# A spectral layer and a rational MLP on one core: batch 0's x in halves of 48 rows, its results stored per two chunks, a fifth chunk of batch 1 ahead of the main loop

## The chip, the cores and the metric

One core of a Trainium2 chip runs the whole kernel. The metric is device time in microseconds (us), from a launch of the program. Engines: PE (TensorE, the matmuls), ACT (ScalarE), DVE (VectorE), POOL (GpSimd) and SP (SyncE, here only an issuer of DMAs). "Idle before, releaser" in a row is how long the engine stood still ahead of an instruction, and whose end let it go on.

## The reference

```python
X = np.fft.rfft(x, axis=1)                    # x: 4 batches x 3008 x 256, float32
Yr = Xr @ w_r - Xi @ w_i + b_r                # 256 x 256 weights
Yi = Xr @ w_i + Xi @ w_r + b_i
Y  = sign(Y) * max(|Y| - 0.01, 0)             # real and imaginary part apart
y  = np.fft.irfft(Yr + 1j * Yi, n=3008, axis=1)
h  = y.reshape(12032, 256) @ w_in             # 256 x 2048
P  = a0 + a1*h + a2*h^2 + a3*h^3
Q  = 1 + |b0|*|h| + |b1|*h^2
out = (P / (Q + 1e-6)) @ w_out                # 2048 x 256
```

## The kernel before

The transform of length 3008 is split into 47 x 64. For a batch, `f1_task` (L160 ff.) does the 47-point part in eight chunks: a chunk of x (`xin`, 128 partitions, of which 0 to 47 hold group g=0 and 64 to 111 group g=1) goes through eight matmuls (L165), ACT copies the half of group 0 and DVE that of group 1 out of PSUM into a tile `a` (`copy`, L148 and L150), and `send` (L190) stores the tile to the staging tensor `s1` in DRAM, which the trace calls `s`. `f2_task` (L223) reads s1 back as `b_all` (batch 0) or `bt` (batches 1 to 3) and does the 64-point part; `m_task` (L252, L259) mixes with w_r and w_i and thresholds; `i1_task` (L277) starts the inverse transform and stores to a second staging tensor `s2` (row `s<-zt`); `i2_task` (L323) ends it from tiles `ct` and leaves its result as `xsh` (ACT, L326) and `xsl` (DVE, L334).

The program has two parts. The **prologue** (L506 to the line `pro_stack.close()`) is batch 0's transform up to i1, with the conversion of the MLP's weights, which come as float64 words (`raw_win`, `raw_wsp`; `convert`, L490 to L502), woven in by hand through the lists `HC`, `HM` and `HF`. `warm` issues matmuls on an unused tile (L517); `WARM` of them stand between batch 0's f1 and f2. At the end of the prologue four f1 chunks of batch 1 are done: one in the last round of the loop over p, three in the loop over `HF`, each followed by some steps of `convert`. Their stores (`sends`, then `direct`) stand in SP's queue behind the last loads of ct.

The **main loop** runs over 208 units. A unit is h (`g1_mm`, L357), the rational function on ACT (v, s, t in L389 to L393, y in L398 and L400), DVE (t in L405 and L406, g in L414 and L426, v in L416) and POOL, with a DMA that adds s to v (L391), and the second product `g2_mm` (acc, L447) of the unit three back. The transforms of batches 1 to 3 are laid between the units by a planner: `fft_tasks` gives each task a cost in us, and a task is taken when what has been spent falls behind a budget.

All of the kernel's order is written by hand (`manual_schedule`): each engine and each DMA queue works in the order of issue. An instruction waits on semaphores for what it reads, and for old users of a buffer that it writes. The DMAs that SP and ACT issue take eight completion counters (DMAHW0 to DMAHW7) in turn, and a DMA waits for the last one on its counter.

The tiles of the prologue lie in pools (`pro`, `pro2`, `pro3`) that are closed before the main loop; the loop's pools `mx` (xsh, xsl) and `mp` (v, s, t, y, g) take over their memory, so a first write there waits for the last users of what lay there.

Of the kernel before, what the change touches and what calls it, by code (L numbers as in the profile page):

```python
# [28 lines left out]
WARM = 27  # L29
HC = (0, 0, 3, 3, 3, 3, 3, 3, 3, 3, 3, 3)  # L30
HM = (0, 0, 3, 4, 3, 4, 3, 4, 3, 4, 3, 4, 8, 0)
HF = (2, 3, 2)
I2Q = (5, 6)
SIZES = (5,) * 14 + (4,) + (5,) * 10 + (4,)
C0 = float(np.float32(1.0) + np.float32(1e-6))
# [59 lines left out]
def spectral_moe(ctx, tc, t, out):  # L95
# [37 lines left out]
    def load_x(b, c):  # L133
        if b == 1 and c in (2, 3):
            xt = pro3.tile([128, 4, D], F32, tag=f"x{c}", name="xin", bufs=1)
        elif b == 1 and c >= 6:
            xt = sm.tile([128, 6, D], F32, tag="x", name="xin", bufs=2)[:, :4]
        elif b == 0 and c >= 2:
            xt = const.tile([128, 4, D], F32, tag=f"win{c}", name="xin")
        else:  # L140
            xt = sm.tile([128, 4, D], F32, tag="xin", name="xin")
        rows = 112 if b == 0 and c < 2 else 128
        nc.sync.dma_start(out=xt[:rows], in_=t["x"][b, c, :rows])
        xin[b, c] = xt

    def copy(eng, out, in_):
# [12 lines left out]
    def f1_task(b, c, pos):  # L159
        if pos == 0:  # L160
            s1[b] = dram.tile([NK, 2, NG, NJ, D], F32, tag="s1", name="s1")
        pts = [bank(b, "f1" if g else "") for g in range(NG)]
        for g, h in ((0, 0), (1, 1), (0, 1), (1, 0)):
            r = slice(64 * g, 64 * g + 48)
            nc.tensor.matmul(out=pts[g][64 * h:64 * h + 64], lhsT=f1[r],  # L165
                             rhs=xin[b, c][r, 2 * h:2 * h + 2, :].rearrange("p j d -> p (j d)"), start=True, stop=True)
        yield
        whole = None
        if b == 0:
            whole = const.tile([128, NG, 2, D], F32, tag=f"wsp{c}", name="a")  # L170
        elif early:
            whole = pro.tile([128, NG, 2, D], F32, tag="a" if pos < 3 else "wt", name="a", bufs=3 if pos < 3 else 1)
        elif b > 1:
            whole = sm.tile([128, 3, 2, D], F32, tag="x", name="a", bufs=2)[:, :NG]
        parts = [sm.tile([128, 2, D], F32, tag="a", name="a", bufs=3) if whole is None else whole[:, g] for g in range(NG)]
        for g in range(NG):
            copy(g if early else b == 1, parts[g].rearrange("p j d -> p (j d)"), pts[g])
        yield
        del xin[b, c]
        if b == 1 and c < 2:  # L180
            hold.append(lambda: load_x(b, c + 4))
        elif b > 1 and c + 2 < NJ // 4:
            load_x(b, c + 2)
        dst = s1[b].rearrange("k c g j d -> (k c) g j d")

        def send():
            for h in range(2):
                r, o = slice(64 * h, 64 * h + 48), slice(4 * c + 2 * h, 4 * c + 2 * h + 2)
                if whole is not None:
                    nc.sync.dma_start(out=dst[:, :, o], in_=whole[r])  # L190
                else:
                    for g in range(NG):
                        nc.sync.dma_start(out=dst[:, g, o], in_=parts[g][r])

        send() if b == 0 or direct or not early else sends.append(send)

    sends = []
    direct = []
    b_t = {}
# [258 lines left out]
    def drain(g):  # L458
        for _ in g:
            pass  # L460

    def fft_tasks(b):
        turns = (0, 1, 2, 3, 6, 7, 4, 5) if b == 1 else range(8)
        ts = [(0.87, 2, 2, f1_task(b, c, pos), 0) for pos, c in enumerate(turns)]
        ts += [(0.0, 0, 0, load_first(b), 0)] + [(0.0, 0, 0, iter(()), 0)]
        np_ = NK // 2
        for p in range(np_ + 2):
            if p < np_:
                ts.append((0.86, 1, 1, f2_task(b, p), 1))
            if p == 0:  # L470
                ts.append((0.0, 0, 0, iter(()), 0))
            if 1 <= p <= np_:
                ts += [(1.43, 1 - k, k, m_task(b, p - 1, k), 0) for k in range(2)]
            if p >= 2:
                ts.append((0.87, 1, 1, i1_task(b, p - 2), 0))
        return ts
# [29 lines left out]
    with tc.manual_schedule():  # L506
        nc.vector.memset(cb, 1.0)
        nc.scalar.dma_start(out=f1, in_=t["f1"])
        nc.scalar.activation(out=cb, in_=cb, func=ACTF.Abs_reciprocal_sqrt)
        b_all = [pro3.tile([128, 6, D], F32, tag=f"b{z}", name="b_all", bufs=1) for z in range(4)]  # L510
        nc.vector.memset(offset[:, 0], 0.0)
# [5 lines left out]
                nc.tensor.matmul(out=pt, lhsT=idle[:, :128], rhs=idle, start=True, stop=True)  # L517

        warm(9)
        for c in range(8):  # L520
            load_x(0, c)
        sel = pro.tile([4, 130], F32, tag="sel", name="sel", bufs=1)
        bsb = pro.tile([4, D], F32, tag="bsb", name="bsb", bufs=1)
        blo = pro.tile([4, D], F32, tag="blo", name="blo", bufs=1)
        eye = pro.tile([128, 128], F32, tag="eye", name="eye", bufs=1)

        def load_small():
            nc.sync.dma_start(out=sel, in_=t["sel"])
            for k, nm in enumerate(("b_r", "b_i")):
                nc.sync.dma_start(out=bsb[2 * k:2 * k + 2, :],  # L530
                                  in_=t[nm].rearrange("(o d) -> o d", o=1).to_broadcast([2, D]))
            nc.sync.dma_start(out=eye, in_=t["minus"])

        def prepare_small():
            nc.vector.memset(v32(selr), 0.0)
            nc.vector.memset(v32(bias), 0.0)
            yield
            nc.vector.tensor_copy(selr[:4], sel[:, 0:128])
            nc.scalar.activation(out=minus, in_=eye, func=ACTF.Copy)
            bhi = bias[:4, 0]  # L540
            nc.vector.tensor_copy(bhi, bsb)
            yield
            nc.vector.tensor_tensor(out=blo, in0=bsb, in1=v32(bhi), op=ALU.subtract)
            nc.vector.tensor_scalar(out=bsb, in0=v32(bhi), scalar1=sel[:, 128:129], scalar2=None, op0=ALU.mult)
            yield
            for k in range(2):
                nc.vector.scalar_tensor_tensor(out=bias[:4, k], in0=blo, scalar=sel[:, 129:130], in1=bsb, op0=ALU.mult, op1=ALU.add)
# [41 lines left out]
        def load_f2(a, z):  # L589
            nc.sync.dma_start(out=f2[:, a:z], in_=f2_src[:, a:z])  # L590
# [8 lines left out]
            nc.sync.dma_start(out=wt, in_=t["w"])  # L599
            wts.extend(wt[:, k] for k in range(2))  # L600

        load_small()
        small_steps = prepare_small()
        for c in range(8):
            drain(f1_task(0, c, c))
            if c >= 4:
                next(small_steps, None)
        load_f2(0, 8)
        load_wt()
        prepare_mix()  # L610
        load_all(0, 2)
        load_all(2, 2)
        load_all(4, 2)
        load_f2(8, 12)
        np_ = NK // 2
# [5 lines left out]
        for p in range(np_ + 3):  # L621
            if p < np_:
                f2g = f2_task(0, p)
                next(f2g)
                next(f2g)
            if p < 2:
                warm(2 - p, "m")
            flush()
            if p == np_:
                load_first_c(0, 16)  # L630
            if p == np_ + 2:
                load_first_c(16, NK - 2)
            if p == 0:
                more_raw(2)
            elif p == 1:
                load_all(12, 6)
            elif p == 2:
                load_f2(12, 24)
                nc.sync.dma_start(out=ca, in_=t["a"].rearrange("(o d) -> o d", o=1).to_broadcast([128, 4]))
                nc.sync.dma_start(out=cb, in_=t["b"].rearrange("(o d) -> o d", o=1).to_broadcast([128, 2]))  # L640
                nc.sync.dma_start(out=i2, in_=t["i2"])
            if p >= 1:
                more_raw(2)
            if p == 3:
                load_g1(8, 16)
            elif p == 4:
                load_all(18, 6)
            elif p == 5:
                load_g1(16, NK)
            if 6 <= p < 12:  # L650
                load_x(1, (0, 1, 2, 3, 6, 7)[p - 6])
            if p < np_:
                convert(HC[p])
            if p == np_ + 1:
                drain(i1_task(0, p - 3))
                root()
            if 2 <= p < np_ + 2:
                drain(m_task(0, p - 2, 0))
                drain(m_task(0, p - 2, 1))
                convert(HM[p])  # L660
            if p < np_:
                drain(f2g)
            if p == np_ + 1:
                drain(first.pop(0)[3])
            if p >= 3 and p != np_ + 1:
                drain(i1_task(0, p - 3))
            if p == 8:
                for k, nm in enumerate(("b_r", "b_i")):
                    for z in range(2):
                        nc.sync.dma_start(out=offset[64 * k:64 * k + 64, z],  # L670
                                          in_=t[nm].rearrange("(o d) -> o d", o=1).to_broadcast([64, D]))
# [148 lines left out]
```

## Time and profile before

| | us |
|---|---|
| median of 3 runs | 1435.2 (1434.85 to 1436.17) |
| the profiled execution, its own time | 1433.67 |
| its span, first to last instruction | 1431.9 |
| PE busy | 1400.0 (98%) |
| DVE busy | 1295.3 (90%) |
| ACT busy | 1133.3 (79%) |
| POOL busy | 669.0 (47%) |

The span is 1.8 us shorter than the execution's own time, and that is 1.5 us under the median of the runs. Busy shares are means over the whole span; the first 155 us look different from the rest, and all that is changed lies there.

### The profile page before, as it was taken

What the parts mean: (1) busy time and instruction counts of PE and PEld (TensorE: products, weight loads), DVE (VectorE), ACT (ScalarE), POOL (GpSimd) and SP (SyncE); (2) the same over time, 40 slices, a digit from 0 to 9 for tenths busy, and PEclk for the clock granted to TensorE, in tenths of its full rate; (3) what the DMA queues carried; (4) which work ended last, traced back from release to release, by engine and by line L of the source; (5) the groups of instructions that cost most, each with busy time, mean ns of one, the idle gap of its engine ahead of it and who ended that gap; (6) DMA issues with size and microseconds to landing.
All of it is one profiled execution on the core that took longest, in us unless ns stands there. A gap on an engine that the chain in (4) does not pass through costs nothing.

```text
span 1431.9 us, 20413 instructions
## 1 busy us (share of the span) xinstructions
PE 1400.0 (98%) x7552; PEld 1227.9 (86%) x7553; DVE 1295.3 (90%) x1302; ACT 1133.3 (79%) x1435; POOL 669.0 (47%) x444
## 2 busy tenths in 40 slices
PE   6989999999999999999999999999999999999997
PEld 2976899998888999999878999999988888888886
DVE  2778889999889889999889899999999999999998
ACT  2767777878888778878788787888788998889985
POOL 0443344454454444444444444455455555555553
PEclk8999999999999999999999999999999999999999
DMA  8968455546586554564686455554555555555543
GB/s 283 385 197 198 99 110 125 107 102 143 134 212 150 104 122 100 105 147 98 132 227 148 97 126 113 114 121 96 103 119 114 108 109 105 112 109 108 109 84 79
DMA packets 85079, 191.66 MB, mean 134 GB/s; under 512 B 8748, under 2 KB 40468, under 8 KB 84980
## 3 DMA queue, kind: packets, MB, share of 16 engines
q0 software_dynamic: 29952, 98.58, 38.7%
q1 hardware_dynamic: 54884, 91.75, 19.4%
q8 instruction: 60, 0.98, 0.3%
q14 instruction: 39, 0.32, 0.1%
q10 hardware_dynamic: 144, 0.03, 0.0%
HBM read 54.28 MB, written 37.49 MB: 64 GB/s over the span
## 4 chain that ended last, share of the span: by engine, by line
PE 77%; DVE 11%; issue 8%; DMA 2%; ACT 2%; SPq 1%; DVEq 0%; ACTq 0%
PE h L357 30%; PE acc L447 29%; PE pft L259 7%; PE pi L323 3%; DVE t L405 3%; DVE v L416 3%; PE pft L223 3%; PE pft L277 2%; PE pft L165 1%; DVE g L414 1%; DMA s<-a 1%; PE pm L259 1%; DVE t L406 1%; DVE e L497 1%; DVE e L495 1%
## 5 line engine op out<-in xcount | busy, mean ns | idle before, releaser
L447 PE MATMUL acc<-g,wsp 128*128 128x470 f32 (+1 forms) x2496 | 561.1, 373 | 4.7 <-DVE g L426 4.7
L420 POOL TENSOR_TENSOR t<-t,v 128x940 f32<-128x940 f32 (+1 forms) x206 | 477.3, 2317 | 139.5 <-DVE v L416 126.8
L447 PEld LDWEIGHTS acc<-g,wsp 128*128 128x128 f32 x2496 | 468.4, 189 | 64.1 <-DVE g L426 6.0
L357 PE MATMUL h<-xsh,win 128*128 128x470 f32 (+1 forms) x1664 | 433.6, 382 | 5.4 <-DVE t L406 4.9
L391 POOL DMA_DIRECT2D v<-s x208 | 183.8, 884 | 535.5 <-issue 498.3
L357 PEld LDWEIGHTS h<-xsh,win 128*128 128x128 f32 x1664 | 303.9, 190 | 60.9 <-PE acc L447 9.6
L389 ACT ACTIVATE v<-h 128x940 f32<-128x940 f32 (+1 forms) x208 | 196.1, 943 | 150.7 <-PE h L357 144.5
L414 DVE SCALAR_TENSOR_TENSOR g<-t,small,y 128x940 fp32r<-128x940 f32 (+1 forms) x208 | 253.6, 1219 | 53.1 <-ACT y L400 52.8
L405 DVE TENSOR_TENSOR t<-t,h 128x940 f32<-128x940 f32 (+1 forms) x208 | 231.3, 1112 | 24.9 <-ACT t L393 23.2
L406 DVE SCALAR_TENSOR_TENSOR t<-t,small,h 128x940 f32<-128x940 f32 (+1 forms) x208 | 245.1, 1179 | 7.4
L426 DVE SCALAR_TENSOR_TENSOR g<-t,small,y 128x940 fp32r<-128x940 f32 (+1 forms) x208 | 244.1, 1174 | 0.1
L357 PE MATMUL h<-xsl,win 128*128 128x470 f32 (+1 forms) x832 | 242.4, 373 | 0.0
L416 DVE SCALAR_TENSOR_TENSOR v<-v,g 128x940 f32<-128x940 f32 (+1 forms) x208 | 231.6, 1113 | 0.0
L393 ACT ACTIVATE t<-h,small 128x940 f32<-128x940 f32 (+1 forms) x208 | 215.7, 1037 | 0.0
L398 ACT ACTIVATE y<-v 128x940 f32<-128x940 f32 (+1 forms) x208 | 205.6, 989 | 9.7 <-DMA v<-s 9.4
L400 ACT ACTIVATE y<-y 128x940 f32<-128x940 f32 (+1 forms) x208 | 204.1, 981 | 2.4
L390 ACT ACTIVATE s<-h 128x940 f32<-128x940 f32 (+1 forms) x208 | 195.2, 939 | 0.0
L357 PEld LDWEIGHTS h<-xsl,win 128*128 128x128 f32 x832 | 156.3, 188 | 20.1
L259 PE MATMUL pft<-wrh,x 128*128 128x256 f32 x288 | 76.5, 287 | 0.2 <-ACT pft L150 0.2
L259 PE MATMUL pft<-wih,x 128*128 128x256 f32 x288 | 75.3, 283 | 0.1
L323 PEld LDWEIGHTS pi<-small,ct 96*128 96x128 f32 x512 | 65.0, 192 | 5.9 <-ACT a L150 3.1
L323 PE MATMUL pi<-small,ct 96*128 96x94 f32 x512 | 64.2, 272 | 2.3 <-DMA ct<-s 2.2
(88 smaller groups left out, 1065.8 us busy)
## 6 DMA issues: line engine op xcount, KB each, us to landing
v<-s POOLq DMA_DIRECT2D x192, 470.0 KB, 4.6
xin<-in_x SPq DMA_DIRECT2D x30, 512.0 KB, 6.2
s<-zt SPq DMA_DIRECT2D x48, 256.0 KB, 3.5
out_t<-ob SPq DMA_DIRECT2D x48, 235.0 KB, 4.4
s<-a SPq DMA_DIRECT2D x56, 192.0 KB, 4.3
ct<-s SPq DMA_DIRECT2D x20, 480.0 KB, 5.6
bt<-s SPq DMA_DIRECT2D x36, 256.0 KB, 3.8
v<-s POOLq DMA_DIRECT2D x16, 376.0 KB, 4.2
```

Of the source, the lines that this page charges most:

```text
L259: nc.tensor.matmul(out=pt[:, k, :], lhsT=l, rhs=r, start=False, stop=n == len(ops) - 1, skip_group_check=True)
L357: nc.tensor.matmul(out=h[:, i, :w], lhsT=l, rhs=r, start=k == 0, stop=k == len(halves) // FU - 1)
L393: nc.scalar.activation(out=d["t"], in_=h, func=ACTF.Identity, scale=rate["a3"], bias=ca[:, 2:3])
L398: nc.scalar.activation(out=d["y"], in_=d["v"], func=ACTF.Square, bias=C0)
L400: nc.scalar.activation(out=d["y"], in_=d["y"], func=ACTF.Abs_reciprocal_sqrt)
L405: nc.vector.tensor_tensor(out=tt, in0=tt, in1=h, op=ALU.mult)
L406: nc.vector.scalar_tensor_tensor(out=tt, in0=tt, scalar=ca[:, 1:2], in1=h, op0=ALU.add, op1=ALU.mult)
L414: stt(out=hi, in0=tt, scalar=ca[:, 0:1], in1=y, op0=ALU.add, op1=ALU.mult)
L416: stt(out=v, in0=v, scalar=C0, in1=v32(hi), op0=ALU.add, op1=ALU.mult)
L420: nc.gpsimd.tensor_tensor(out=tt[:, :cut], in0=tt[:, :cut], in1=v[:, :cut], op=ALU.subtract)
L426: stt(out=lo, in0=tt, scalar=ca[:, 0:1], in1=y, op0=ALU.add, op1=ALU.mult)
L447: nc.tensor.matmul(out=acc[n][e][:, :w], lhsT=l, rhs=r, start=begun[n] == 1 and seen[e] == 1, stop=begun[n] == UB and seen[e] == 3 * FU)
```

## The change

1. Batch 0's x is loaded as sixteen halves of 48 rows (192 KB each), twelve from SP's queue and four (group 1 of chunks 0 to 3) from ACT's, ahead of ACT's table load. Before, it came as eight loads of 112 or 128 rows from SP.
2. Batch 0's results are stored per two chunks, group by group, from 48 partitions with 4 KB a row: eight stores on SP (group 1) and eight on ACT (group 0). Before there were sixteen on SP with rows of 2 KB. The host lays x out to fit.
3. The small inputs `sel`, `b_r`, `b_i` are loaded by ACT after the f1 stage, and what DVE makes of them follows then. `eye` is loaded at p == 2, and ACT's copy of it to `minus` moves to p == 6.
4. Behind the stores SP's order becomes f2 table 0 to 3, b_all 0 and 1, wt, b_all 2 and 3, f2 table 4 to 7, b_all 4 and 5, f2 table 8 to 11; `prepare_mix` comes after f2 of p == 0.
5. A fifth f1 chunk of batch 1 is done in the loop over HF (2, 2, 2, 1). Its tile `a` lies in pool `pro3` under the tag "x".
6. The planner's cost of an f1 task is 0.95, and in the last two chunks of batch 1 both copies are ACT's.

```diff
-HF = (2, 3, 2)
+HF = (2, 2, 2, 1)
...
-        rows = 112 if b == 0 and c < 2 else 128
-        nc.sync.dma_start(out=xt[:rows], in_=t["x"][b, c, :rows])
+        if b == 0:
+            for g in range(NG):
+                r = slice(64 * g, 64 * g + 48)
+                (nc.scalar if g and c < 4 else nc.sync).dma_start(out=xt[r], in_=t["x"][b, c, r])
+        else:
+            nc.sync.dma_start(out=xt, in_=t["x"][b, c])
...
+        pair, s = divmod(c, 2)
         if b == 0:
-            whole = const.tile([128, NG, 2, D], F32, tag=f"wsp{c}", name="a")
+            if not s:
+                a_t[:] = [const.tile([128, 2, 2, D], F32, tag=f"wsp{2 * pair + g}", name="a") for g in range(NG)]
+        elif early and pos == 4:
+            whole = pro3.tile([128, 3, 2, D], F32, tag="x", name="a")[:, :NG]
...
-            copy(g if early else b == 1, parts[g].rearrange("p j d -> p (j d)"), pts[g])
+            copy(g if early else b == 1 and pos < 6, parts[g].rearrange("p j d -> p (j d)"), pts[g])
...
+        if b == 0:
+            for g, h in ((g, h) for g in range(NG) for h in range(2) if s):
+                o = 8 * pair + 4 * h
+                (nc.sync if g else nc.scalar).dma_start(
+                    out=dst[:, g, o:o + 4], in_=a_t[g][64 * h:64 * h + 48].rearrange("p s j d -> p (s j) d"))
+            return
...
-        send() if b == 0 or direct or not early else sends.append(send)
+        send() if direct or not early else sends.append(send)
...
-        ts = [(0.87, 2, 2, f1_task(b, c, pos), 0) for pos, c in enumerate(turns)]
+        ts = [(0.95, 2, 2, f1_task(b, c, pos), 0) for pos, c in enumerate(turns)]
...
-        load_small()
-        small_steps = prepare_small()
         for c in range(8):
             drain(f1_task(0, c, c))
-            if c >= 4:
-                next(small_steps, None)
-        load_f2(0, 8)
+        load_small()
+        drain(prepare_small())
+        load_f2(0, 4)
+        load_all(0, 2)
         load_wt()
-        prepare_mix()
-        load_all(0, 2)
         load_all(2, 2)
+        load_f2(4, 8)
         load_all(4, 2)
         load_f2(8, 12)
```

Three places in the order show what moves. In these rows a number behind a name is a buffer's own, and a wait on "Activation", "DVE" or "PE" is one for that engine's work.

SP at the start of the program, before: the last loads of x, the small loads, and the first four of sixteen stores.

```order
L143 DMA xin_121<-in_x 128x1024
L143 DMA xin_123<-in_x 128x1024 [waits DMAHW0_49]
L528 DMA sel_125<-in_sel 4x130 [waits DMAHW1_49]
L530 DMA bsb_126<-in_b_r 2x256 [waits DMAHW2_49]
L530 DMA bsb_126<-in_b_i 2x256 [waits DMAHW3_49]
L532 DMA eye_128<-in_minus 128x128 [waits DMAHW4_49]
L190 DMA s1_133<-a_140 96x1x512 [waits DMAHW5_49,DVE_49,Activation_49]
L190 DMA s1_133<-a_140 96x1x512 [waits DMAHW6_49]
```

SP at the same place in the change: the loads of chunks 6 and 7 and SP's eight stores.

```order
L145 DMA xin_111<-in_x 48x1024 [waits DMAHW7_49]
L145 DMA xin_111<-in_x 48x1024 [waits DMAHW1_49]
L145 DMA xin_114<-in_x 48x1024 [waits DMAHW3_49]
L145 DMA xin_114<-in_x 48x1024 [waits DMAHW4_49]
L200 DMA s1_137<-a_145 48x1024 [waits DMAHW6_49,DVE_49]
L200 DMA s1_137<-a_145 48x1024 [waits DMAHW0_49]
L200 DMA s1_137<-a_167 48x1024 [waits DMAHW2_49,DVE_49]
L200 DMA s1_137<-a_167 48x1024 [waits DMAHW4_49]
L200 DMA s1_137<-a_189 48x1024 [waits DMAHW6_49,DVE_49]
L200 DMA s1_137<-a_189 48x1024 [waits DMAHW1_49]
L200 DMA s1_137<-a_211 48x1024 [waits DMAHW2_49,DVE_49]
L200 DMA s1_137<-a_211 48x1024 [waits DMAHW3_49]
```

The first load of chunk 7 (`xin_114`) now stands on counter 3, whose last user is ACT's first store (below, `a_144`), and all of SP's stores stand behind that load. The seventh and eighth rows of stores wait on counters that ACT's last stores use.

ACT at the start of the change; before, the only DMA in this queue was the one of f1, and no store.

```order
L145 DMA xin_102<-in_x 48x1024 [waits DMAHW0_49]
L531 ACT_TABLE_LOAD
L531 ACTIVATE small_69<-small_69 128x2 [waits DVE_49]
L154 ACTIVATE a_144<-pft_138 128x512 [waits PE_49]
L154 ACTIVATE a_144<-pft_148 128x512 [waits PE_49]
L200 DMA s1_137<-a_144 48x1024 [waits DMAHW3_49,Activation_49]
L200 DMA s1_137<-a_144 48x1024 [waits DMAHW5_49]
L154 ACTIVATE a_166<-pft_160 128x512 [waits PE_49]
```

The copies of chunks 0 and 1 (`a_144`) now come ahead of a store that ACT itself issues, and the copies of chunk 2 (`a_166`) behind it.

ACT at the end of the prologue, before: the copy of the fourth chunk, the last conversion, the first xsh of the main loop, and the first v.

```order
L150 ACTIVATE a_1073<-pft_1067 128x512 [waits PE_49]
L502 ACTIVATE wsp7_1079<-e_1046 128x2x256 [waits DVE_49]
L326 ACTIVATE xsh_1091<-pi2_1093 128x470 [waits DMAHW2_49,DMAHW4_49,DMAHW0_49,PE_49]
L326 ACTIVATE xsh_1091<-pi2_1099 128x470 [waits PE_49]
L389 ACTIVATE v_1146<-h_1113 128x940 [waits DMAHW3_49,DMAHW4_49,DMAHW2_49,DMAHW5_49,DMAHW1_49,DMAHW6_49,DMAHW0_49,DMAHW7_49,PE_49,Pool_49]
```

The same place in the change, with the fifth chunk's copy (`a_1096`).

```order
L154 ACTIVATE a_1081<-pft_1075 128x512 [waits PE_49]
L522 ACTIVATE wsp7_1088<-e_1055 128x2x256 [waits DVE_49]
L154 ACTIVATE a_1096<-pft_1090 128x512 [waits PE_49]
L346 ACTIVATE xsh_1111<-pi2_1113 128x470 [waits DMAHW1_49,DMAHW3_49,DMAHW0_49,DMAHW5_49,DVE_49,DMAHW7_49,PE_49,Activation_49]
L346 ACTIVATE xsh_1111<-pi2_1119 128x470 [waits PE_49]
```

And SP's last rows of the prologue in the change; before, the row of a_1073 was the last of eight stores.

```order
L209 DMA s1_1020<-a_1081 96x1x512 [waits DVE_49,Activation_49]
L209 DMA s1_1020<-a_1081 96x1x512 [waits DMAHW6_49]
L209 DMA s1_1020<-a_1096 96x1x512 [waits DMAHW7_49,DVE_49,Activation_49]
L209 DMA s1_1020<-a_1096 96x1x512 [waits DMAHW0_49]
L147 DMA xin_1129<-in_x 128x1024 [waits DMAHW1_49,PE_49]
```

The two stores of `a_1096` are the last users of counters 7 and 0 ahead of the main loop, and the first xsh waits on both of these; before, the xsh waited for none of the f1 stores of batch 1, and the first v (L389) did.

## Rows read from the trace of the kernel before

**Rows 1.** The page: the chain that ended last, shares by engine.
```profile
PE 77%; DVE 11%; issue 8%; DMA 2%; ACT 2%; SPq 1%; DVEq 0%; ACTq 0%
```

**Rows 2.** The chain of waits, 0 to 60 us: start, length, what.
```profile
8.16 6.75 DMA bsb<-in_b_i
...
24.04 4.01 DMA s<-a
28.20 3.67 DMA b_all<-s
...
32.01 2.04 PE pft L223 x8
...
38.27 2.88 PE pm L259 x24
```

**Rows 3.** The timeline of PE, first 25 us: start, length, instructions, idle before them.
```profile
14.70 1.09 PE L165 MATMUL pft<-xin,small 48*64 48x512 f32 x8 [0.20 <-DMA xin<-in_x]
15.98 5.99 PE L517 MATMUL pft<-offset 128*128 128x512 bf16 x26 [0.19 <-ACT a L150]
```

**Rows 4.** The timeline of ACT, 0 to 40 us.
```profile
8.22 0.60 ACT L150 ACTIVATE a<-pft 128x512 f32<-128x512 f32 x1 [0.58 <-PE pft L165]
...
39.07 0.68 ACT L490 ACTIVATE e<-raw_win 128x512 f32<-128x512 f32 x1 [0.40 <-DMA raw_win<-in_w_in]
```

**Rows 5.** Tile a, 0 to 40 us: ns min/median/max of an issue; time to landing.
```profile
L190 SPq DMA_DIRECT2D s<-a x16: 547/680/1321, 10.8 to 24.0; - x16
...
DMA to landing us min/median/max: 2.9/3.5/4.0
```

**Rows 6.** Tile zt, 30 to 100 us: stores of 256 KB.
```profile
DMA to landing us min/median/max: 2.1/2.1/2.1
```

**Rows 7.** Windows: busy time of each engine, granted clock, DMA share, GB/s.
```profile
8.00:10.00 2.00, 1.70 (x16) 0.47 (x16) 1.24 (x2) 1.19 (x2) 0.00 (x0) 1.00 1.02 408
20.00:22.00 2.00, 1.97 (x10) 0.69 (x7) 0.00 (x0) 0.00 (x0) 0.00 (x0) 1.00 0.87 223
24.00:26.00 2.00, 0.00 (x0) 0.00 (x0) 0.00 (x0) 0.00 (x0) 0.00 (x0) 1.00 0.86 262
26.50:27.00 0.50, 0.00 (x0) 0.00 (x0) 0.00 (x0) 0.00 (x0) 0.00 (x0) 0.89 0.79 160
32.00:37.00 5.00, 4.99 (x20) 4.42 (x21) 2.27 (x4) 1.30 (x3) 0.00 (x0) 0.50 0.98 314
105.50:108.50 3.00, 3.00 (x8) 2.14 (x8) 0.73 (x2) 0.52 (x1) 0.08 (x1) 0.50 0.86 260
120.00:152.00 32.00, 29.86 (x148) 24.79 (x147) 31.79 (x33) 24.77 (x29) 15.41 (x10) 0.95 0.73 158
152.00:252.00 100.00, 99.77 (x574) 90.98 (x573) 86.29 (x91) 77.53 (x99) 40.80 (x27) 1.00 0.50 112
```

**Rows 8.** The timeline of SP, 90 to 140 us: issues.
```profile
101.10 5.96 SPq L190 DMA_DIRECT2D s<-a  x8
```

**Rows 9.** The chain of waits, 94 to 170 us.
```profile
105.86 4.05 DMA s<-a
110.18 0.95 ACT v L389
...
128.88 1.28 DVE a L148 x2
```

**Rows 10.** The timeline of PE, 94 to 160 us.
```profile
102.98 2.44 PE L323 MATMUL pi<-small,ct 96*128 96x94 f32 x20 [2.22 <-DMA ct<-s]
105.21 3.59 PE L357 MATMUL h<-xsh,win 128*128 128x470 f32 x8
108.59 1.13 PE L357 MATMUL h<-xsl,win 128*128 128x470 f32 x4
```

**Rows 11.** The timeline of ACT, 98 to 160 us.
```profile
104.34 0.56 ACT L326 ACTIVATE xsh<-pi 128x470 fp32r<-128x470 f32 x1
```

**Rows 12.** The timeline of DVE, 104 to 160 us.
```profile
119.86 1.20 DVE L414 SCALAR_TENSOR_TENSOR g<-t,small,y 128x940 fp32r<-128x940 f32 x1 [1.03 <-ACT y L400]
```

More of the change, by code (lines that the diff above doesn't have):

```diff
@@ L174, in f1_task @@
             whole = sm.tile([128, 3, 2, D], F32, tag="x", name="a", bufs=2)[:, :NG]
-        parts = [sm.tile([128, 2, D], F32, tag="a", name="a", bufs=3) if whole is None else whole[:, g] for g in range(NG)]
+        if b == 0:
+            parts = [a[:, s] for a in a_t]
+        else:
+            parts = [sm.tile([128, 2, D], F32, tag="a", name="a", bufs=3) if whole is None else whole[:, g] for g in range(NG)]
         for g in range(NG):
-            copy(g if early else b == 1, parts[g].rearrange("p j d -> p (j d)"), pts[g])
+            copy(g if early else b == 1 and pos < 6, parts[g].rearrange("p j d -> p (j d)"), pts[g])
         yield
@@ L184, in f1_task @@
         dst = s1[b].rearrange("k c g j d -> (k c) g j d")
+        if b == 0:
+            for g, h in ((g, h) for g in range(NG) for h in range(2) if s):
[3 more added lines that the diff above has]
+            return
         def send():
             for h in range(2):
-                r, o = slice(64 * h, 64 * h + 48), slice(4 * c + 2 * h, 4 * c + 2 * h + 2)
+                o = 8 * pair + 4 * h + 2 * s
+                r, o = slice(64 * h, 64 * h + 48), slice(o, o + 2)
                 if whole is not None:
@@ L193, in send @@
                         nc.sync.dma_start(out=dst[:, g, o], in_=parts[g][r])
-        send() if b == 0 or direct or not early else sends.append(send)
+        send() if direct or not early else sends.append(send)
+    a_t = []
     sends = []
@@ L508, in spectral_moe @@
         nc.scalar.dma_start(out=f1, in_=t["f1"])
+        for c in range(8):
+            load_x(0, c)
         nc.scalar.activation(out=cb, in_=cb, func=ACTF.Abs_reciprocal_sqrt)
@@ L519, in spectral_moe @@
         warm(9)
-        for c in range(8):
-            load_x(0, c)
         sel = pro.tile([4, 130], F32, tag="sel", name="sel", bufs=1)
@@ L527, in load_small @@
         def load_small():
-            nc.sync.dma_start(out=sel, in_=t["sel"])
+            nc.scalar.dma_start(out=sel, in_=t["sel"])
             for k, nm in enumerate(("b_r", "b_i")):
-                nc.sync.dma_start(out=bsb[2 * k:2 * k + 2, :],
+                nc.scalar.dma_start(out=bsb[2 * k:2 * k + 2, :],
                                   in_=t[nm].rearrange("(o d) -> o d", o=1).to_broadcast([2, D]))
-            nc.sync.dma_start(out=eye, in_=t["minus"])
         def prepare_small():
@@ L538, in prepare_small @@
             nc.vector.tensor_copy(selr[:4], sel[:, 0:128])
-            nc.scalar.activation(out=minus, in_=eye, func=ACTF.Copy)
             bhi = bias[:4, 0]
@@ L641, in spectral_moe @@
                 nc.sync.dma_start(out=i2, in_=t["i2"])
+                nc.sync.dma_start(out=eye, in_=t["minus"])
             if p >= 1:
@@ L662, in spectral_moe @@
                 drain(f2g)
+            if p == 0:
+                prepare_mix()
+            elif p == 6:
+                nc.scalar.activation(out=minus, in_=eye, func=ACTF.Copy)
             if p == np_ + 1:
@@ L802 @@
     for g in range(NG):
-        xp[:, :, g * 64:g * 64 + N2] = x.reshape(B, N2, NG, NJ // 4, 4, D)[:, :, g].swapaxes(1, 2)
+        xg = x.reshape(B, N2, NG, NJ // 8, 2, 2, 2, D)[:, :, g]
+        xp[:, :, g * 64:g * 64 + N2] = xg.transpose(0, 2, 4, 1, 3, 5, 6).reshape(B, NJ // 4, N2, 4, D)
     arrays = {"x": xp, **dft_tables()}
```

## The prediction

> **What bounds the kernel now.** I read the page first: the chain that ended last is PE for 77% of the span [rows 1], so only stretches where PE stands still can give or lose time, unless matmuls go. Windows by stage show where that is: between 152 and 252 us PE is busy for 99.77 of 100 us, while from 120 to 152 us it is DVE that has no gap (31.79 of 32 us) [rows 7]. So what the change moves counts up to about 152 us; behind that the program is solid PE work, and a shift that reaches 152 us stays to the end. The chain of waits then names the waits of the two stretches. In the first, 0 to 60 us: the small load of b_i holds DVE's copies until 14.9; the last store is issued at 24.04 and takes 4.01 us, b_all another 3.67, and PE takes up f2 at 32.01 [rows 2]. [...] The mixing starts at 38.27 [rows 2]. In the second stretch, 100 to 120 us, SP issues the eight f1 stores of batch 1 from 101.10 to 107.06 [rows 8], the last lands at 109.91, and the first v waits for it until 110.18 [rows 9]. PE meanwhile has the inverse transform and the first h: it works, at clock 0.50 again [rows 7, 10].
>
> **The change part by part.**
>
> *Start (loads, stores, small inputs).* The DVE copies lose the wait for b_i. The f1 stage was fed by loads at 408 GB/s [rows 7], the stores by one queue at 0.68 us per issue (median of sixteen) [rows 5]. With two queues, issue is no longer the limit. What the new order makes of it is a chain of landings: the first load of chunk 7 stands on a counter whose last user is ACT's first store, and SP's stores stand behind that load. I walk it. ACT's copy of chunk 1 ends at 8.22 + 0.60 = 8.82 [rows 4]; its store goes out at 8.85. How long does such a store take? The trace has no 48-row store of 4 KB rows; the nearest are the old stores from 48 partitions, 192 KB like these, with 2.9 to 4.0 us and a median of 3.5 [rows 5], and stores of 256 KB that run nearly alone, 2.1 [rows 6]. I take 3.3, nearer to the former, and keep 2.1 and 4.0. So chunk 7's load goes out at 12.15, lands at 15.45, its matmuls take 1.09 [rows 3] and end near 16.6 (before: 14.70 + 1.09 = 15.79). ACT's copy takes 0.6 (17.2), its store 3.3 (20.5). SP's third last store waits on that store's counter; the two behind it follow in issues of 0.6 each (21.7), and the last lands at 25.0. Then b_all, 3.67 and 0.14 to PE's start: f2 at about 28.8 instead of 32.01, **3.2 us earlier**. With 2.1 for all landings f2 starts near 24.3 (7.7 earlier), with 4.0 near 31.6 (0.4 earlier).
>
> [...]
>
> What follows is fed by loads. The f2 table is split, and its second 256 KB now stand behind the stores, where the old first 512 KB had been moved mostly before. 256 KB at 314 GB/s [rows 7] are 0.8 us, so the first raw weights, which ACT meets at 39.07 after 0.40 us of waiting [rows 4], come only some 2.3 earlier. The conversion chain on ACT and DVE leads from there to the end of the prologue. Between 3.2 and 2.3 I take **−2.8 us**. The copy to minus now sits in that chain at p == 6, one ACT instruction of 0.3 us and perhaps a wait: **+0.2** (0 to 0.5). The small loads and their DVE work lie under the stores and b_all (19 to 28 us), where DVE has nothing else; without that cover they would cost their chain of about 3 us. Moving prepare_mix behind f2 of p == 0 costs nothing while wt lands before PE's third f2.
>
> *End of the prologue (fifth chunk).* Its eight matmuls (1.09 us) fit into the 2.22 us in which PE waits for ct [rows 10], so they are free. Its stores are not. There are now ten in SP's queue at 5.96 / 8 = 0.745 each [rows 8]: the tenth goes out at 101.10 + 9 × 0.745 = 107.8 and lands 3.5 to 4.05 later, at 111.3 to 111.9 (times of before, the shift of the start apart). Its tile lies where the loop's first xsh is written, so ACT's first xsh, which stood at 104.34 [rows 11], waits for that landing: about 111.5, +7.2. Behind xsh stand xsl, all of h(0), the v of unit 0 and everything of the loop. PE idles from 105.4 to 112.4 and finds its clock at 0.50. h(0) took 105.21 to 109.72 [rows 10] at that clock; now it ends at about 116.9 and v comes at 117.0 instead of 110.18, since it waits for matmuls and no longer for the stores: +6.8. DVE's first g, 119.86 [rows 12], comes at 126.6, **+6.7**. From there DVE is the bound. Given back: two pairs of copies of 1.28 us each [rows 9] leave DVE for ACT, but DVE waits for ACT's y in the same units, so I take 1.3 of these 2.56 us (bounds 0 and 2.56). f2 of batch 1 comes a unit earlier, with two DVE operations in the full stretch: +0.5 (0 to 0.5). One f1 task fewer is left for the solid part: −1.0. Net 6.7 − 1.3 + 0.5 − 1.0 = **+4.9 us**; bounds 2.4 (landing 2.9, all copies gained, f2 free) and 8.
>
> *The planner's cost* of 0.95 for 0.87 shifts tasks of batches 2 and 3 by fractions of a unit in solid PE work: 0.
>
> *Sum.* −2.8 + 0.2 + 4.9 = **+2.3 us**. The profiled execution took 1433.67 (span 1431.9), 1.5 under the median of 1435.2; added to the median that makes **1437.5**, +0.16%. A measurement of this kernel can hardly tell less than 0.2% (2.9 us) from no change, so the forecast is "same", on the slow side.
>
> **The rivals.**
>
> *Clock kept.* [...] Chance 0.15.
>
> *Fifth chunk hidden.* Should the stores land before xsh is due, the end of the prologue gains: −1.3 on DVE, −1.0 on PE, no wait. Sum −2.8 + 0.2 − 2.3 = −4.9: 1430.3, faster. It would need the ten landings by 104.3, 7 us sooner than worked out; only if the copies of f1 came much before the last ct load, behind which the stores stand. Chance 0.12.
>
> *Slow halves.* Everything that moves now moves from or to 48 partitions. With 128 rows the loads ran at 408 GB/s; the old stores from 48 ran at 223 to 262 [rows 7]. If that was the partitions and not the issue of 0.745 us per 192 KB (which alone makes 264 GB/s, so the trace can't tell the two apart), 3.1 MB of loads and 3.1 MB of stores at 240 GB/s take 26 us from 1.7 on: the last lands at 28, as before (24.04 + 4.01), and the start gives nothing. Sum 0 + 0.2 + 4.9 = +5.1: 1440.3, slower. It decides as soon as the mean rate up to the last store is under some 260 GB/s. Chance 0.20.
> [...]
>
> *Circular waits.* The two queues wait for each other through the eight counters. With 4.0 per landing the chain above gains 0.4, f1 ends later than before, and the sum is −0.4 + 0.2 + 4.9 = +4.7: 1439.9, slower. For it: the top of [rows 5]. Against: fewer packets. Chance 0.10.
>
> **How the numbers follow.** Forecast 0.43, its own range 1434 to 1440.5; clock kept 0.15, fifth chunk hidden 0.12, slow halves 0.20, circular waits 0.10. Faster than 1432.3: the hidden chunk and part of clock kept, with a little of the forecast's lower end, 0.21. Slower than 1438.1: the last two and a third of the forecast, with the rest of both at the bound, 0.39. Same: 0.40. The range runs from the hidden chunk, somewhat inside, to slow halves with the upper bounds of the end: 1431 to 1441.5.
>
> **What would show it.** Right: the chain of waits has an ACT store, chunk 7's load and one of SP's last stores between 9 and 25 us, f2 starts between 28 and 29.5 at clock 0.50; ACT's first xsh stands 6 to 8 us behind PE's pi with a releaser "DMA s<-a", PE idles there, and the first v waits for PE. Wrong: f2 before 27 or at full clock; xsh released by PE or ct; f1 matmuls in gaps of more than 3 us; a conversion chain that does not move with f2; or a loop that has made up the late start by 155 us.

## The result, and the profile after

The changed kernel takes 1444.23 us (median of four, 1442.49 to 1445.51), the kernel before 1435.68 in the same comparison: a ratio of 1.0058 (95% interval 1.0041 to 1.0075), so 8.3 us slower (5.9 to 10.8). It lies above the range that was given. The profiled execution took 1442.49 us, 8.8 more than that of before.

The page of the change: span, busy time, and the chain that ended last.

```profile
span 1440.7 us, 20421 instructions
PE 1405.0 (98%) x7553; PEld 1231.2 (85%) x7553; DVE 1296.1 (90%) x1297; ACT 1134.8 (79%) x1440; POOL 668.0 (46%) x444
PE 74%; DVE 9%; issue 8%; DMA 5%; ACT 3%; SPq 0%; ACTq 0%; DVEq 0%
```

PE has the same matmuls and 5 us more busy time (before: 1400.0), and 5% of the chain is DMA instead of 2% [rows 1]. The chain of waits, first 60 us (start, length, what):

```profile
1.66 5.90 DMA xin<-in_x
...
9.36 4.75 DMA s<-a
...
14.13 3.54 DMA xin<-in_x
...
17.81 2.56 PE pft L169 x8
...
20.98 3.93 DMA s<-a
...
25.74 3.40 DMA s<-a
...
29.33 2.77 DMA b_all<-s
...
32.23 2.05 PE pft L243 x8
...
36.77 12.48 DMA raw_win<-in_w_in
```

This is the chain that was walked ahead: ACT's first store, chunk 7's load behind it, ACT's last store, SP's last store, b_all. But each link is longer or later, and f2 starts at 32.23, where it started at 32.01 [rows 2]. Windows of the change show why the f1 stage crawls (columns as in [rows 7]):

```profile
8.00:10.00 2.00, 1.52 (x16) 0.31 (x8) 0.69 (x1) 0.60 (x1) 0.00 (x0) 1.00 1.12 217
10.00:12.00 2.00, 1.11 (x13) 0.34 (x8) 0.69 (x1) 0.60 (x1) 0.00 (x0) 1.00 1.00 184
18.00:20.00 2.00, 2.00 (x8) 0.23 (x6) 0.00 (x0) 0.00 (x0) 0.00 (x0) 0.84 0.94 299
20.00:22.00 2.00, 2.00 (x8) 0.63 (x6) 1.32 (x3) 0.60 (x1) 0.00 (x0) 0.50 0.79 232
```

The DMA engines are as busy as before (share 1.0 and over) and move 184 to 217 GB/s where they moved 408. PE stood still between chunks, and its clock fell in the stage itself, to 0.50 at 20 to 22 us. The timeline of PE shows what that did to the last chunk (1.09 us before) and to the warm-up behind it (5.99 before, [rows 3]):

```profile
17.81 2.51 PE L169 MATMUL pft<-xin,small 48*64 48x512 f32 x8 [0.94 <-DMA xin<-in_x]
20.26 7.23 PE L539 MATMUL pft<-offset 128*128 128x512 bf16 x27
32.23 2.05 PE L243 MATMUL pft<-f,b_all 128*128 128x128 f32 x8 [4.75 <-DMA b_all<-s]
```

The timeline of ACT has the first raw weights and the start of the main loop:

```profile
40.31 0.67 ACT L510 ACTIVATE e<-raw_win 128x512 f32<-128x512 f32 x1 [1.86 <-DMA raw_win<-in_w_in]
...
111.49 1.02 ACT L346 ACTIVATE xsh<-pi 128x470 fp32r<-128x470 f32 x2 [6.51 <-DMA s<-a]
116.30 0.95 ACT L409 ACTIVATE v<-h 128x940 f32<-128x940 f32 x1 [3.80 <-issue]
```

The raw weights come 1.2 us later than in [rows 4], though in this execution the prologue has made that up at its end (SP's stores start at 101.05, before at 101.10, [rows 8]). Then the first xsh stands 6.51 us for a store of batch 1: 111.49 instead of 104.34 [rows 11]. SP and PE at the same place:

```profile
101.05 7.47 SPq L209 DMA_DIRECT2D s<-a  x10
```

```profile
112.10 3.25 PE L377 MATMUL h<-xsh,win 128*128 128x470 f32 x8 [4.63 <-ACT xsh L346]
```

To follow a shift through the loop I read the start of ACT's first instruction of each of the 208 units (v) from the timelines of both kernels and took the difference; a step in it is a place where time is lost or won. The rows of the experiments, told below, stand in the same table:

```
unit                        0       2      20      40      64     112     207
before, us             110.18  119.73  249.45  384.13  548.33  868.03 1412.32
the change              +6.12   +6.81   +6.52   +6.52   +8.36   +8.78   +8.78
e1_start_only           +4.07   +4.86   +4.87   +4.87   +5.10   +5.10   +5.12
e2_cost_only            +0.31   +0.41   +0.40   +0.40   +0.50   +2.30   +2.31
e3_cost_old            +10.77  +11.31  +12.46  +12.47  +13.44  +14.14  +14.19
e4_fifth_elsewhere      +3.31   +3.77   +4.99   +4.99   +6.00   +6.52   +6.51
e5_halves_only          +3.63   +3.42   +3.43   +3.43   +3.75   +4.13   +4.14
e6_full_rows            -2.79   -2.17   -2.17   -2.17   -2.04   -1.35   -1.29
e7_full_fifth_else      -1.46   -0.76   -0.87   -0.86   +0.13   +0.78   +0.82
e8_columns              +2.25   +2.61   +2.62   +2.61   +2.73   +3.29   +3.27
e9_whole_rows_in_change +2.09   +2.57   +2.17   +2.17   +3.19   +3.88   +3.87
e10_dve_copies          -0.65   +0.05   -1.09   -1.08   -0.89   -0.42   -0.45
```

A row is one execution; the execution of before that was profiled, 1433.67, is among the fastest of its kind (those beside e1 to e4 have a median of 1435.81), so all differences are some 2 us high, and the ratios of the timed runs have the last word on a size.

In the change 6.8 of the 8.8 us are there at unit 2 and 6.5 at unit 40; the other 2.3 come in steps behind unit 40. One of them is a wait of batch 2's first f2 for its input. The chain of waits of the change there:

```profile
447.32 4.35 DMA s<-a
451.75 5.19 DMA bt<-s
457.07 1.13 PE pft L243 x8
```

A wait of the same kind stands ahead of the first f2 of batch 1, in the timeline of PE:

```profile
139.96 1.13 PE L243 MATMUL pft<-f,bt 128*128 128x128 f32 x8 [1.23 <-DMA bt<-s]
```

In the kernel before PE waits for bt in neither place. What this takes back shows when DVE's first g of a unit (L414 before, L434 in the change) is followed from unit 0 to unit 2; before, then the change:

```profile
132.35 1.19 DVE L414 SCALAR_TENSOR_TENSOR g<-t,small,y 128x940 fp32r<-128x940 f32 x1
```

```profile
126.67 1.20 DVE L434 SCALAR_TENSOR_TENSOR g<-t,small,y 128x940 fp32r<-128x940 f32 x1 [1.53 <-ACT y L420]
137.70 1.19 DVE L434 SCALAR_TENSOR_TENSOR g<-t,small,y 128x940 fp32r<-128x940 f32 x1
```

Unit 0's g is 6.81 us late (119.86 before, [rows 12]), unit 2's only 5.35: the copies taken from DVE give back 1.46. At unit 20 the change is 6.52 late again, 1.17 more, and PE has waited 1.23 for bt in between. The same reckoning for the kernels with a fifth chunk, and for e6, which has none (differences to the kernel before, us):

```
                          g of unit 0  g of unit 2  v of unit 20  PE's wait for bt
the change                      +6.81        +5.35         +6.52              1.23
e3_cost_old                    +11.31        +9.85        +12.46              2.66
e4_fifth_elsewhere              +3.77        +2.31         +4.99              2.73
e7_full_fifth_else              -0.76        -2.22         -0.87              1.39
e9_whole_rows_in_change         +2.57        +1.11         +2.17              1.13
e10_dve_copies                  +0.06        -1.14         -1.09                 0
e6_full_rows                    -2.17        -2.17         -2.17                 0
```

In each row what is lost between the g of unit 2 and the v of unit 20 is the wait, to within 0.1 us. (e10 keeps both engines' copies in the last two chunks; the other four with a loss leave them to ACT, as the change does.)

### The profile page after: what moved, and what is told of

The parts are those of the page before. It is cut to its first block, busy times and chain, and to the rows that moved or that the text cites. A ratio compares the mean times of both kernels' runs of the same rounds, so it can differ in the third digit from the quotient of the medians.

```text
span 1440.7 us, 20421 instructions
## 1 busy us (share of the span) xinstructions
PE 1405.0 (98%) x7553; PEld 1231.2 (85%) x7553; DVE 1296.1 (90%) x1297; ACT 1134.8 (79%) x1440; POOL 668.0 (46%) x444
## 4 chain that ended last, share of the span: by engine, by line
PE 74%; DVE 9%; issue 8%; DMA 5%; ACT 3%; SPq 0%; ACTq 0%; DVEq 0%
PE h L377 29%; PE acc L467 28%; PE pft L279 7%; PE pi L343 4%; DVE t L425 3%; DVE v L436 3%; PE pft L243 2%; PE pft L297 2%; PE pft L169 1%; DMA raw_win<-in_w_in 1%; DMA s<-a 1%; DMA v<-s 1%; DVE g L434 1%; DMA xin<-in_x 1%; DMA bt<-s 1%
## 5 line engine op out<-in xcount | busy, mean ns | idle before, releaser
L434 DVE SCALAR_TENSOR_TENSOR g<-t,small,y 128x940 fp32r<-128x940 f32 (+1 forms) x208 | 256.4, 1232 | 55.2 <-ACT y L420 53.8
```

The source lines that it names most:

```text
L434: stt(out=hi, in0=tt, scalar=ca[:, 0:1], in1=y, op0=ALU.add, op1=ALU.mult)
```

## The experiments

All ratios are to the kernel before, run in turn with each on the same chip; one hundredth of a per cent is 0.14 us.

**The start alone (e1_start_only).** The change with these three undone:

```diff
-HF = (2, 2, 2, 1)
+HF = (2, 3, 2)
-        ts = [(0.95, 2, 2, f1_task(b, c, pos), 0) for pos, c in enumerate(turns)]
+        ts = [(0.87, 2, 2, f1_task(b, c, pos), 0) for pos, c in enumerate(turns)]
-            copy(g if early else b == 1 and pos < 6, ...)
+            copy(g if early else b == 1, ...)
```

> The change's parts 1 to 4 alone (x in halves, paired stores, late small inputs); the old HF, the old cost 0.87, both engines' copies as before. Theory (the three parts add up: start 0, fifth chunk +6.5, cost +2.3): f2 of batch 0 starts at 32.0 to 32.5 us as in the change and in the kernel before, first xsh at 104 to 105, time within 1.5 us of before. Rival (the late xsh comes from the start's new order, through later stores or conversions): first xsh past 108 and at least +4 us.

Measured: 1.0009 (0.9997 to 1.0021), +1.3 us (-0.4 to +3.0), within what the theory allowed; but its runs spread from 1434.5 to 1440.1, and their median of 1438.81 is 3.0 above that of before. In the profiled one f2 starts at 31.84, its first xsh at 107.11, between the two expectations; the raw weights come at 41.70 (39.07 before). The start gains nothing, and in part of its runs it loses.

**The cost alone (e2_cost_only).** The kernel before with 0.95 for 0.87.

> The kernel before with the planner's cost of an f1 task at 0.95 and nothing else. Theory (the cost moves f1 tasks of batches 2 and 3 late enough that f2 waits for bt): +2.3 us, shown as a step between units 40 and 60 and a smaller one near unit 108. Rival (the steps come from the late start of the loop, which leaves the planner's order out of step): no change, within 0.5 us.

Measured: 0.9991 (0.9981 to 1.0001), -1.3 us. The theory falls: no loss is shown. Its profiled execution does have a step of 1.8 us between units 64 and 112, yet the runs are not slower than those of before.

**The change with the old cost (e3_cost_old).** The change with 0.87.

> The change with the planner's cost back at 0.87. Theory: 2.3 us faster than the change, so +6.5 over before, and the distance of its units to those of before stays flat at about 6.5 from unit 20 to the end. Rival (late start, not cost): +8.8 as the change, with steps near units 45 to 55.

Measured: 1.0044 (1.0030 to 1.0058), +6.3 us, as expected by the theory in size, but the interval overlaps that of the change, and the table denies its reason: the steps behind unit 40 are there (12.47 to 14.19) with the old cost too. So e2 and e3 both speak against the cost as the source of the steps; the 2 us are the difference of two uncertain ratios. Its profiled execution is the slowest of its runs (1447.9, median 1443.75): f2 came at 34.30.

**The fifth chunk in other memory (e4_fifth_elsewhere).** The change, but the fifth chunk's tile is not in pool pro3:

```diff
-        elif early and pos == 4:
-            whole = pro3.tile([128, 3, 2, D], F32, tag="x", name="a")[:, :NG]
-        elif early:
+        elif early and pos < 4:
             whole = pro.tile(...)
```

> The change with the fifth chunk's two halves in tiles of a pool that stays open (tag a, 2 KB a partition each, four stores of 48 rows instead of two of 96), so that the first xsh writes to memory no store of it reads. Theory (the reuse of memory is the whole loss at the loop's start): first xsh at 104 to 105, first v at 110 to 111 behind the eight stores, 6 us faster than the change: +2 to +3 over before. Rival (the four more rows in the queue and the fewer idle slots delay the loop whatever the memory): first v past 113, and +6 or more.

Measured: 1.0011 (1.0001 to 1.0021), +1.6 us: 6.7 us faster than the change. The timeline of ACT of this run:

```profile
106.15 0.55 ACT L344 ACTIVATE xsh<-pi 128x470 fp32r<-128x470 f32 x1
108.50 0.56 ACT L344 ACTIVATE xsh<-pi 128x470 fp32r<-128x470 f32 x1 [1.80 <-PE pi L341]
113.49 0.95 ACT L407 ACTIVATE v<-h 128x940 f32<-128x940 f32 x1 [4.43 <-PE h L375]
```

No xsh waits for a store any more. The first xsh and the first v stand later than expected (104 to 105, 110 to 111), and the first v is past the rival's 113, though the time is not the rival's +6. This execution is the slowest of its ten (1440.61, median 1438.47), its raw weights came at 41.34, 1.0 later than in the change, and it waits 2.73 for bt; so its row in the table shows less of the gain than the runs do. That the wait comes from the reused memory is shown, and by the runs it is most of the loss: 6.7 us, a difference of two ratios that are each known to some 2 us.

**Halves alone (e5_halves_only).** The kernel before with the change's `load_x`, all else old.

```diff
-        rows = 112 if b == 0 and c < 2 else 128
-        nc.sync.dma_start(out=xt[:rows], in_=t["x"][b, c, :rows])
+        if b == 0:
+            for g in range(NG):
+                r = slice(64 * g, 64 * g + 48)
+                (nc.scalar if g and c < 4 else nc.sync).dma_start(out=xt[r], in_=t["x"][b, c, r])
+        else:
+            nc.sync.dma_start(out=xt, in_=t["x"][b, c])
```

> The kernel before with only the loads of batch 0's x changed to halves of 48 rows (twelve on SP, four on ACT); its sixteen stores on SP and all else as before. No store stands ahead of a load's counter here. Theory (halves move slowly by themselves, 180 to 260 GB/s): f1 matmuls show gaps for xin of 0.3 us and more and the last chunk's matmuls start past 15.5, at 16 to 17; time 0 to +2 us over before. Rival (the circular wait of chunk 7 on ACT's first store is what made f1 late): the last chunk starts at 14.7 as before, no change.

Measured: 1.0034 (1.0021 to 1.0047), +4.9 us, more than either expectation. Windows and PE's timeline of this run:

```profile
8.00:10.00 2.00, 1.30 (x12) 0.45 (x15) 0.84 (x2) 0.60 (x2) 0.00 (x0) 1.00 1.07 191
10.00:12.00 2.00, 2.00 (x15) 0.56 (x13) 0.70 (x2) 0.65 (x2) 0.00 (x0) 1.00 1.04 211
```

```profile
19.30 5.99 PE L521 MATMUL pft<-offset 128*128 128x512 bf16 x26
35.53 2.05 PE L227 MATMUL pft<-f,b_all 128*128 128x128 f32 x8 [10.24 <-DMA b_all<-s]
```

No store is issued before 15.4 us, and the loads move 191 to 211 GB/s. The f1 matmuls end at about 19.3 instead of 15.8, and f2 follows 3.5 us late. In the change they end at 20.3, and 1.4 us of that is the last chunk's slow clock (2.51 for 1.09). So the wait of chunk 7 for ACT's store can hardly be what made f1 late; it was not tried by itself.

**Whole pieces with the rest of the start (e6_full_rows).** The start alone as in e1, but x loaded in eight whole pieces from SP (the lines of before in `load_x`).

> The start of the change (paired stores from two queues, late small inputs, new order of loads) with x loaded in eight whole pieces from SP as before; no fifth chunk, cost 0.87. Theory (the halves and the chunk 7 wait behind them ate the gain of the stores): f1 ends near 15.9, the last store lands near 22 to 24, f2 starts at 26 to 28, the first raw weights land at 35 to 37; 3 to 5 us faster than before. Rival (the stores from 48 rows at 223 to 262 GB/s are the limit whatever the loads): f2 at 30 or later and no change.

Measured: 0.9981 (0.9972 to 0.9991), 2.7 us faster than before (1.3 to 4.0), just under the expected 3 to 5; f1 ended at 16.9 and the last store landed at 24.5, both a little later than expected. Windows, PE and ACT of this run:

```profile
10.00:12.00 2.00, 1.78 (x16) 0.24 (x8) 0.88 (x2) 1.07 (x2) 0.00 (x0) 1.00 1.03 410
14.00:16.00 2.00, 1.04 (x12) 0.20 (x8) 0.72 (x2) 0.60 (x1) 0.00 (x0) 1.00 1.03 414
20.00:22.00 2.00, 2.00 (x11) 0.88 (x9) 0.00 (x0) 0.00 (x0) 0.00 (x0) 1.00 0.88 250
```

```profile
27.86 1.76 PE L239 MATMUL pft<-f,b_all 128*128 128x128 f32 x8 [5.01 <-DMA b_all<-s]
```

```profile
36.30 0.68 ACT L506 ACTIVATE e<-raw_win 128x512 f32<-128x512 f32 x1 [2.41 <-DMA raw_win<-in_w_in]
```

Loads and the first stores together move 410 GB/s; once only stores are left (20 to 22 us) it is 250, no more than the 223 to 262 of the old stores [rows 7], though two queues issue them. f2 starts 4.15 us earlier and the raw weights land 2.8 earlier; it is the latter that reaches the loop (-2.79 at unit 0). Against e1 the only edit is the halves: 4.0 us.

**And the fifth chunk in other memory (e7_full_fifth_else).** e6 with the edit of e4, HF (2, 2, 2, 1), and ACT copying both halves of the last two chunks.

> As the run with whole pieces of x, and with the fifth chunk of batch 1 in the prologue in tiles of the pool that stays open, ACT copying both halves of the last two chunks; cost 0.87. Theory (the fifth chunk is nearly free once its tile does not hold up xsh): within 1.5 us of the run without the fifth chunk, so 2 to 5 us faster than before. Rival (four more stores ahead of the loop cost as much as one task saves): 2 us or more slower than the run without it.

Measured: 0.9986 (0.9976 to 0.9996), 0.7 us slower than e6, inside the 1.5. So the fifth chunk brings nothing even where xsh does not wait for it. Here too PE stands still ahead of the first f2 of batch 1:

```profile
132.55 1.13 PE L237 MATMUL pft<-f,bt 128*128 128x128 f32 x8 [1.39 <-DMA bt<-s]
```

**Half the columns (e8_columns).** As e5, but the halves are columns over all rows: `out=xt[:rows, j], in_=t["x"][b, c, :rows, j]` with two of four j in each.

> The kernel before with x of batch 0 in sixteen loads again, twelve on SP and four on ACT, but each half is half of the columns over all 112 or 128 rows (rows of 2 KB) instead of 48 rows of 4 KB. Theory (48 partitions make the load slow, not the number or size of the loads): 350 to 410 GB/s between 6 and 14 us, last chunk's matmuls start at 14.5 to 15.5, f2 within 0.7 us of 32.0, no change in time. Rival (sixteen small loads on two queues are slow whatever their rows): 190 to 260 GB/s, f1 ends near 19 and f2 near 35.5, +4 to +5 us.

Measured: 1.0017 (1.0007 to 1.0026), +2.4 us: between the two. Its windows and PE's timeline:

```profile
8.00:10.00 2.00, 1.23 (x8) 0.39 (x8) 0.07 (x1) 0.11 (x1) 0.00 (x0) 1.00 0.93 341
10.00:12.00 2.00, 0.40 (x5) 0.31 (x8) 0.62 (x1) 0.49 (x1) 0.00 (x0) 1.00 0.95 305
14.00:16.00 2.00, 2.00 (x12) 0.72 (x8) 0.83 (x2) 0.74 (x2) 0.00 (x0) 0.50 0.83 274
```

```profile
11.68 8.84 PE L170 MATMUL pft<-xin,small 48*64 48x512 f32 x46 [1.60 <-DMA xin<-in_x]
34.09 2.05 PE L228 MATMUL pft<-f,b_all 128*128 128x128 f32 x8 [7.64 <-DMA b_all<-s]
```

With all partitions sixteen loads move 305 to 341 GB/s, against 191 to 211 in e5 and 408 for whole pieces. These rates count every byte, and a quarter of a whole piece of 128 rows is rows that no matmul reads (the matmuls take 48 + 48). Of rows that are read, whole pieces bring 306 GB/s, the columns 229 to 256, the halves 191 to 211. So both the 48 rows and the division into sixteen cost rate, and neither theory alone holds; which is the larger part depends on what is counted. (The columns' rows are 2 KB, those of the 48-row halves 4 KB; that difference was not taken apart.)

The time does not divide them either. Behind a gap of 1.60 us PE's clock is at 0.50 from 14 to 20 us in this execution, and f1 ends at 20.5, later than in e5, whose clock stays at 1.00: a part of the 2.4 us is the clock and not the loads.

**The change with whole pieces (e9_whole_rows_in_change).** One edit to the change: `load_x` as before.

> The change with one edit: x in whole pieces from SP. Fifth chunk in its old tile, cost 0.95. Theory (parts add up): f2 at 27.5 to 29, the raw weights at 36 to 37, so 4 us faster than the change up to the end of the prologue; the xsh wait is still 6 to 7 us; in all +3.5 to +5 over before. Rival (an earlier prologue only lets SP reach the stores earlier, so the wait shrinks too, or the loop takes back the gain): +1.5 or less, or +7 or more.

Measured: 1.0026 (1.0013 to 1.0039), +3.7 us: 4.6 us faster than the change, as expected. f2 starts at 27.48, and the wait is still there in the timeline of ACT:

```profile
107.39 1.02 ACT L342 ACTIVATE xsh<-pi 128x470 fp32r<-128x470 f32 x2 [6.55 <-DMA s<-a]
```

**DVE's copies back (e10_dve_copies).** e7 with `copy(g if early else b == 1, ...)`.

> As the run with whole pieces and the fifth chunk in the open pool, but the last two chunks of batch 1 are copied by ACT and DVE as before, not by ACT alone. Theory (ACT, not DVE, sets the loop's first units, so two copies more on ACT delay y and with it DVE): 0.7 to 2 us faster than that run, at or under the run without a fifth chunk. Rival (f2 waits for bt, whatever engine copies): within 0.5 us of it.

Measured: 0.9980 (0.9970 to 0.9989), 2.9 us faster than before and 0.9 than e7, but the intervals of the two overlap. The theory's reason is not what the traces show. In the same stretch of the program, from unit 0's v to unit 3's, ACT is the busier engine with its copies (13.78 of 15.74 us in e7, DVE 10.61) and not without them (11.84 of 14.77 in e10, DVE 11.49), but neither engine is full, and DVE's g of unit 2 comes 1.08 us earlier in e7 (130.13) than in e10 (131.21). What the rival names, f2's wait for bt, is what differs, though it does depend on the engine: e10 does not have it.

```profile
132.41 1.05 PE L237 MATMUL pft<-f,bt 128*128 128x128 f32 x8
```

With ACT's copies the loop runs ahead, but the stores do not come ahead with it: SP issues the first load of bt in e7 at 127.99 and in e10 at 128.36, so e7's lead of 1.08 us is spent in a wait of 1.39. Batch 2's first f2 has the same difference (PE waits 1.0 to 1.1 us for bt in the change, e3, e4, e7 and e9, and not at all in e10 and e6). Why that second wait follows the copies of batch 1 is open. From unit 0 to 207 e7 loses 2.28 on before in the table, e10 0.20.

## Why the prediction was wrong, point by point

*The sum.* Forecast: start -2.6, end of the prologue and first units +4.9, cost 0. Measured: start +1.3 (e1, -0.4 to +3.0); the wait of xsh 6.7 (the change against e4; 5.7 between e9 and e7, which also differ in the cost). That leaves some 0.3 of the 8.3 us for all else, with an uncertainty of several us.

*The first step that failed is the start.* The walk through the landings took the f1 stage as fed at the old pace, with only chunk 7 late, and 3.3 us for each landing; that x itself now came from 48 rows was put at nothing in the sum. The links were right, their lengths not: 4.75 for ACT's first store, 3.54 for chunk 7's load, 3.93 and 3.40 for the last stores, 2.51 for the last chunk's matmuls, and f1 ends at 20.3 instead of 16.6. What came was the rival "slow halves", at a chance of 0.20. It had the rate right (240 GB/s forecast; 184 to 262 between 2 and 12 us) and the start's gain of nothing, and it weighed too little because [rows 7] could not tell 48 rows from the issue of the stores. e5 tells it for the loads: the halves alone cost 4.9 us (3.0 to 6.7), of which e8 puts a part on the division into sixteen. e6 tells the rest: the paired stores and the new order, without the halves, are worth 2.7 us, near the 2.6 that the sum had for the start, by an f2 4.15 us earlier and raw weights 2.8 earlier (3.2 and 2.3 forecast).

With as many loads, x came at 191 to 211 GB/s in pieces of 48 rows (e5, 8 to 12 us) and at 305 to 341 in pieces of 112 or 128 (e8, the same windows); why, no run here shows.

*The xsh wait was right.* First xsh at 111.49 (111.5 forecast), held by a store of batch 1, PE idle before h(0), first v waiting for PE and not for stores, DVE's first g at 126.67 (126.6 forecast). The sign and place of the end's loss came from the order of the program and from [rows 8 to 12] alone.

*The second step that failed is what was to be given back.* Forecast: 1.3 us from DVE's copies and 1.0 from the task less, against 0.5 for an earlier f2. The copies gave 1.46 by unit 2. But f2 of batch 1, a unit earlier as forecast, was priced by its DVE operations alone, with no wait for its input: PE stands 1.23 us for bt there, and another 1.04 ahead of batch 2's first f2. So the change is at +6.5 at unit 20, where the forecast had 5.9, and at 8.8 at the end. A gain of 1.0 from the task less is not seen: up to unit 20 nothing is left over beside the wait, and e6, without the fifth chunk, and e10, with it, are 2.7 and 2.9 us faster than before, the same within the noise.

That a shift at 152 us stays to the end did not hold: 2.3 us were added behind unit 40. The waits for bt account for about 1 of them; the rest stays open. Such steps stand in all kernels with the fifth chunk (1.5 to 2.3 us; e10 has 0.6) and in e2, which has no wait for bt, and are 0.2 to 0.9 in the others.

*Cost.* Forecast 0; e2 gives -1.3 (-2.7 to +0.1). Not clear of 0.

*The range* was to run to slow halves with the upper bounds of the end. By the terms as given that is 0 + 0.5 + 8 = +8.5, or 1443.7; it was closed at 1441.5 without a reason, and the measured +8.3 lies between the two.

*The clock.* f2 ran at 0.50 (32.2 to 34.1 us), as forecast; "clock kept" (f2 at the full granted clock, a chance of 0.15) did not come. How long PE stood still before its clock fell was not the same in the two kernels. Before, it fell within 26.5 to 27.0 us [rows 7], some 4.9 us behind the last warm-up matmul (15.98 + 5.99 = 21.97, [rows 3]); in the change between 29.5 and 30.0 us, some 2.1 us behind it (20.26 + 7.23 = 27.49).

```profile
29.50:30.00 0.50, 0.00 (x0) 0.00 (x0) 0.00 (x0) 0.00 (x0) 0.00 (x0) 0.61 0.00 0
```

## What to carry to other kernels

Before a load or store is cut to fewer partitions, look at the DMA share beside the GB/s of windows where that shape already runs. Here the old stores from 48 partitions kept the DMA engines busy to 0.86 and 0.87 at 223 to 262 GB/s [rows 7]: a high share at a low rate could be read as a sign against the issue as the limit, and the loads from 48 rows then bore it out (e5: 191 to 211 GB/s at a share of 1.04 to 1.07). A buffer borrowed from a pool that closes is not free: the first write of its successor waits for its last reader, here 6.51 us for a store at the end of a queue of ten, and everything in the loop stood behind that write. When work is moved off a full engine, follow what it hands on: DVE's gain of 1.46 us was spent in the next wait for a DMA. And compare shifted runs unit by unit, not at the same microsecond: with the loop 7 us late a window from 126 to 135 us holds other units.

Of what was changed, the paired stores, the later small inputs and the new order are worth keeping: with whole pieces of x they run 0.19% faster than before (e6), and with the fifth chunk in open memory and DVE's copies 0.20% (e10); each interval excludes no change.

## What the runs showed of the hardware

The DMA engines were busy to a share of 1.07 at 191 GB/s (e5, loads from 48 rows, 8 to 10 us) and of 1.02 at 408 (the kernel before, whole pieces of the same x, [rows 7]): in these rows the share does not follow the rate. Stores from 48 partitions ran at 250 GB/s with two issuing queues (e6, 20 to 22 us) and at 223 to 262 with one [rows 7].

PE's clock fell inside the f1 stage of the change, where gaps of 0.3 to 0.9 us stood between chunks, to 0.84 at 18 to 20 us and 0.50 at 20 to 22; the last chunk's eight matmuls took 2.51 us for 1.09. In e8 it was at 0.50 from 14 to 20 us, behind gaps of 0.99 and 1.60.
